# A table of issue-order rules per block, a 16-bit AND for |q| and 128-wide weight loads, in a fused attention and gated-GLU kernel

## The chip, the cores and the metric

One core of a Trainium2 chip. The metric is the device time of one execution in microseconds (us). "Ratio" always means the mean time of one kernel's fast runs over that of the other kernel's fast runs of the same rounds, so it is not quite the ratio of the medians that stand beside it.

Engines: PE is TensorE (matmuls), PEld its weight loads, DVE is VectorE, ACT is ScalarE, POOL is GpSimd, SP is the Sync engine, which issues most DMAs.

## The reference

```python
x = A_x                                    # 1 x 2048 x 640, bf16
xn = layernorm(x)
qkv = xn @ wqkv                            # 32 heads of 20
s = softmax(q @ k.T * 20**-0.5) @ v @ wo   # full attention
h = sigmoid(xn @ w_gate) * (xn @ w_up)     # 1728 wide
g = silu(h @ w_down)
return x + s * g
```

## The kernel before

Heads are worked on in groups of four and queries in chunks of 512, which makes 32 blocks. A score job is one 128 x 512 tile of scores of one head; there are 64 x 32 = 2048 of them. Either ScalarE takes a job (an exact exponential, two jobs in one 1024-column instruction from a double bank, if possible a third from a single bank) or VectorE takes it (an integer trick: one `iv` instruction per job, then three passes over groups of four jobs). All other work (projections, the GLU, the output projection) is cut into items and squeezed between the score matmuls.

The issue order of PE, ACT and DVE is fixed when the program is built. A small event model steps through time in 0.02 us, knows each engine's next free time and each buffer's, and at each step decides what to issue. Its rules are constants. This is the core of it, cut:

```python
URGENT, ROUNDS, HOLD, SLACK, LEAD, LAG, D_LAST, D_LAST_END = 0.25, 4, 0.15, 0.2, 40.0, 0.0, 20, 8
D_MAX, SLACKS = 2, (0.2, 0.2)
# ... cut
T_IV, T_ON = 0.605, 0.60                   # the model's VectorE durations
T_PASS = (0.605, 0.605, 1.15)
# ... cut: a fill of the score banks for ACT, and up to two more jobs for DVE
while len(d_new) < D_MAX and (dcur is not None or buf_free(iv_left, NIV)) \
        and busy + T_IV * len(d_new) <= T_F + T_MODE + PL + SLACKS[len(d_new)]:
    f = next((f for f in D_BANKS[own] if flex[f] <= now), None)
    # ... cut: claim a job for DVE, put its score matmul into bank f
third = next((f for f in A_BANKS[own] if flex[f] <= now), None) if len(d_new) < 2 else None
jobs = claim_act(SLOT if third is not None else SLOT - 1, [y[2][2] for y in d_new])
# ... cut: the pick on DVE
pass_ok = dve_pass and (dve_pass[0]["k"] > 0 or buf_free(pb_left, NPB))
if iv_ok and not (dve_last == "iv" and pass_ok and now < dq[0][3] + SLACK):
    nc.vector.tensor_scalar(out=d["iv"][:, j, :], in0=bank[bk], scalar1=B_OFF,
                            scalar2=0.0, op0=ALU.add, op1=ALU.max)
```

For 24 of the 32 heads q and k are projected in units of six heads (120 columns of weights), and a bound on the scores needs |q|:

```python
nc.tensor.matmul(st["ps"][0:UC, :], lhsT=wus[u][:, kd, i, :], rhs=xnT[:, c, kd, :], ...)   # UC = 120
nc.vector.scalar_tensor_tensor(out=aqs[(u, c)][0:UC, :], in0=st["q"], scalar=-1.0, in1=st["q"],
                               op0=ALU.mult, op1=ALU.max)                                  # |q|
```

After the last block a fixed sequence, the tail, divides, projects and stores the last 512 tokens.

Of the kernel before, what the change touches and what calls it, by code (L numbers as in the profile page):

```python
# [12 lines left out]
I16 = mybir.dt.int16  # L13
ACT = mybir.ActivationFunctionType
ALU = mybir.AluOpType
# [3 lines left out]
P = 128  # L19
# [8 lines left out]
UH = 6  # L28
UC = UH * DH

URGENT, ROUNDS, HOLD, SLACK, LEAD, LAG, D_LAST, D_LAST_END = 0.25, 4, 0.15, 0.2, 40.0, 0.0, 20, 8
D_ORD, M_ORD, WAIT3, FALL, M_END = 1, 0, 0.4, 1, 0.3
NPT, NPB, NIV = (3, 7), 3, 3
D_MAX, SLACKS = 2, (0.2, 0.2)
A_BANKS, D_BANKS = ((0, 1, 2), (1, 0, 2)), ((2, 1, 0), (2, 1, 0))
M_BANKS = ((2, 1, 0), (2, 1, 0))

LOG2E = 1.4426950408889634
UNIT = 128.0
# [13 lines left out]
def kernel(  # L53
# [369 lines left out]
    T_F, T_PV, T_MM, T_MODE = 0.2133, 0.2133, 0.2133, 0.107  # L423
    T_IV, T_ON = 0.605, 0.60
    T_PASS = (0.605, 0.605, 1.15)

    def t_exp(n):
        return (0.052 if n < SLOT else 0.104) + 0.4267 * n
# [4 lines left out]
    def gc(b):  # L433
        if b < PAIR:
            return divmod(b, NQC)
        return NG - 2 + (b - PAIR) % 2, (b - PAIR) // 2
# [12 lines left out]
    def mark(*e):  # L449
        return lambda t: ev_at.__setitem__(e, t)  # L450
# [56 lines left out]

    def load_wu(u):
        w = wk.tile([P, 2 * KD, GH, 32], BF16, tag="wp", bufs=2, name="wu")
        w = w.rearrange("p a j e -> p (a j e)")[:, 0:2 * KD * UC].rearrange("p (kd i f) -> p kd i f", i=2, f=UC)  # L510
        f0 = PG * GC + u * UC
        for i in range(2):
            nc.sync.dma_start(out=w[:, :, i, :], in_=wqkv_v[:, :, i, f0:f0 + UC])
        wus[u] = w

    def u_mm(st, u, i, c, kd):
        nc.tensor.matmul(st["ps"][0:UC, :], lhsT=wus[u][:, kd, i, :], rhs=xnT[:, c, kd, :],  # L517
                         start=(kd == 0), stop=(kd == KD - 1))

    def mk_ku(u, c, at):  # L520
# [31 lines left out]
    def mk_qu(u, c, at):  # L552
        st = {}

        def alloc():
            st["ps"] = misc_ps()

        def ab():
            aqs[(u, c)] = wk.tile([P, QC], BF16, tag="aq", bufs=4, name="aq")
            nc.vector.scalar_tensor_tensor(out=aqs[(u, c)][0:UC, :], in0=st["q"], scalar=-1.0, in1=st["q"],  # L560
                                           op0=ALU.mult, op1=ALU.max)

        def ev():
            st["q"] = wk.tile([P, QC], BF16, tag="ku", bufs=2, name="qu")[0:UC, :]
            nc.vector.tensor_scalar_mul(out=st["q"], in0=st["ps"][0:UC, :], scalar1=qscale)
            nc.sync.dma_start(out=qD[u][:, c * QC:(c + 1) * QC], in_=st["q"])
        return Item([("PE", alloc, [(T_MM, lambda kd=kd: u_mm(st, u, 0, c, kd)) for kd in range(KD)]),
                     ("DVE", 0.60, ev, "free", mark("qD", u, c)),
                     ("DVE", 0.60, ab, "", mark("aq", u, c))], at, pre=[("bD", u - 1)] if u else [])

    def mk_bu(u, at):
        st = {}
# [45 lines left out]
    def mk_v(pr, tts, at):  # L618
        st = {}

        def alloc():
            st["ps"] = misc_ps()

        def mm(i, kd):
            nc.tensor.matmul(st["ps"][:, i * 2 * GC:(i + 1) * 2 * GC],  # L625
                             lhsT=xn_tok(tts[i], kd),
                             rhs=wvs[pr][:, kd, :], start=(kd == 0), stop=(kd == KD - 1))

        def done(t):
            for tt in tts:  # L630
                v_at[(pr, tt)] = t
        return Item([("PE", alloc, [(0.08, lambda i=i, kd=kd: mm(i, kd)) for i in range(len(tts)) for kd in range(KD)]),
                     ("DVE", 0.065 + 0.167 * len(tts), lambda: v_evac(st["ps"], pr, tts), "free", done)], at)

    def mk_gu(c, kf, at):
# [244 lines left out]
    def buf_free(left, n):  # L880
        return len(left) < n or (left[len(left) - n][0] == 0 and left[len(left) - n][1] <= now)
# [135 lines left out]
    with tc.manual_schedule(engines={ENG.PE, ENG.Activation, ENG.DVE}):  # L1017
# [17 lines left out]
        dve_last = None  # L1035
        cur = None
        mode = None
        blk_loaded = -1
        active = []
        u_next, k_next, q_next, k_at = 0, PG, PG * NQC, {}  # L1040
# [37 lines left out]
        while chain or items or glu_items or any(it.i < len(it.ops) for it in active):  # L1078
# [2 lines left out]
            bb = base()  # L1081
            if bb > blk_loaded:
                blk_loaded = bb
                g, c = gc(bb)
                if c == 0 and g + 1 < PG:
                    spread_wst(g + 1, load_wst(g + 1))
                if c == 0 and g + 1 < NG:
                    if g % 2 == 1:
                        wvs[(g + 1) // 2] = load_wv((g + 1) // 2)
# [23 lines left out]
            for eng in ("ACT", "DVE"):  # L1113
# [47 lines left out]
                    free["DVE"] = now + 0.16  # L1161
                    continue
                iv_ok = dq and dq[0][3] <= now
                pass_ok = dve_pass and (dve_pass[0]["k"] > 0 or buf_free(pb_left, NPB))
                if iv_ok and not (dve_last == "iv" and pass_ok and now < dq[0][3] + SLACK):
                    dve_last = "iv"
                    d, j, bk, _ = dq.pop(0)
                    nc.vector.tensor_scalar(out=d["iv"][:, j, :], in0=bank[bk], scalar1=B_OFF,  # L1168
                                            scalar2=0.0, op0=ALU.add, op1=ALU.max)
                    end = now + T_IV  # L1170
                    free["DVE"] = end
                    flex[bk] = end + EL
                    d["n"] += 1
                    if d["n"] == len(d["jobs"]) and d is not dcur:
                        dve_pass.append(d)
                elif pass_ok:
                    dve_last = "pass"
                    d = dve_pass[0]
                    k = d["k"]
                    if k == 0:  # L1180
                        d["pb"] = w2.tile([P, 2, GH, QC], BF16, tag="pb", bufs=NPB, name="pb")
                        pb_left.append([2 * len(d["jobs"]), 0.0])
                        d["rel"] = (pb_left, len(pb_left) - 1)
                    passes(d, k)
                    d["k"] += 1
                    end = now + T_PASS[k]
                    free["DVE"] = end
                    if k != 1:
                        for x, (b, kt, j) in enumerate(d["jobs"]):
                            add_unit(b, kt, j, d["pb"][:, k // 2, x, :], k, end + EL, d["rel"])  # L1190
                    if k == 2:
                        dve_pass.pop(0)
                        iv_left[d["i"]][:] = [0, end]
# [13 lines left out]
            if free["PE"] <= now:  # L1207
                s = slots[nfill % 2]
                s_empty = s["a"] is None
                can_f = s_empty and s["ends"] <= now  # L1210
                dry = max(free["ACT"], now) + sum(t_exp(len(x["a"])) for x in slots if x["a"])
                margin = dry - now - (T_F + T_MODE + PL)
                us = [u for u in map(pv_pick, range(GH)) if u is not None] if oacc_at[0] <= now else []
                n_ready = min(sum(u["ready"] <= now and u["b"] == pv_block[0] for u in q) for q in pv_q)
                full = not buf_free(pt_left[3], NPT[1])
                blocked = full or not buf_free(pt_left[2], NPT[0]) or not buf_free(pb_left, NPB)
                pv_ok = len(us) == GH or (len(us) > 0 and (blocked or pv_all(pv_block[0])))
                if cur is None:
                    own = nfill % 2
                    m_new, m_bank = None, None  # L1220
                    m_it = next((e for e in active if e.i < len(e.ops) and e.ops[e.i][0] == "PE" and e.ready <= now), None)
                    if m_it is None:
                        behind = done < due() + LAG
                        for f in ((2,) if not behind and claimed[0] < NJOB * NBLK and not (FALL and not pv_ok and not can_f) else M_BANKS[own]):
                            if flex[f] <= now:
                                m_bank = f
                                break
# [12 lines left out]
                nxt = None  # L1240
                if full and pv_ok:
                    nxt = "PV"
                elif can_f and (margin < URGENT or (stay is None and not (margin > WAIT3 and any(now < flex[f] <= now + WAIT3 for f in A_BANKS[nfill % 2]) and not any(flex[f] <= now for f in A_BANKS[nfill % 2])))):
                    nxt = "F"
                elif stay is not None:
                    nxt = stay
                elif s_empty and s["ends"] <= now + HOLD and mode != "F":
                    nxt = None
                elif pv_ok and (not m_ok or full or (n_ready >= ROUNDS and done >= due() + LAG)):
                    nxt = "PV"  # L1250
                elif m_ok:
                    nxt = "M"
                if nxt == "F":
                    busy = max(0.0, free["DVE"] - now) + T_IV * len(dq)
                    own = nfill % 2
                    d_new = []
                    while len(d_new) < D_MAX and (dcur is not None or buf_free(iv_left, NIV)) \
                            and busy + T_IV * len(d_new) <= T_F + T_MODE + PL + SLACKS[len(d_new)]:
                        f = next((f for f in D_BANKS[own] if flex[f] <= now), None)
                        if f is None:  # L1260
                            break
                        x = claim_dve([t[2] for t in dcur["jobs"]] if dcur else [], [y[2][2] for y in d_new])
# [8 lines left out]
                        flex[f] = 1e9  # L1271
                        if len(dcur["jobs"]) == GH:
                            dcur = None
                    third = next((f for f in A_BANKS[own] if flex[f] <= now), None) if len(d_new) < 2 else None
                    jobs = claim_act(SLOT if third is not None else SLOT - 1, [y[2][2] for y in d_new])
                    if jobs or d_new:
                        for x, t in enumerate(jobs):
# [89 lines left out]
```

## Time and profile before

The median was 839.6 us in three runs.

| | before |
|---|---|
| busy share of ACT, PE, DVE | 96%, 94%, 91% |
| score jobs on DVE | 464 of 2048 |
| first to last exponential | 33.0 to 816.1 us |
| ACT in that stretch: needed + lost | 760.0 + 22.1 us |
| DVE in that stretch: needed + lost | 688.0 + 92.0 us |

"Needed" is an estimate: for every form of instruction on the engine, the 10th percentile of the time from its start to the next start, times its number. "Lost" is what the measured start-to-start times hold above that.

The page's first part gives busy time of each engine (share of the span, number of instructions):

```profile
span 835.7 us, 16970 instructions
...
PE 783.8 (94%) x6388; PEld 277.6 (33%) x6388; DVE 756.3 (91%) x1174; ACT 800.7 (96%) x1043; POOL 81.3 (10%) x90
```

The next view is the sum of busy time over the stretch from 60 to 780 us, in which no start or end effects lie (columns: PE, PEld, DVE, ACT, POOL, each busy us and count, then granted clock, DMA share and GB/s):

```profile
60.00:780.00 720.00, 696.51 (x5687) 239.83 (x5684) 672.46 (x1021) 716.68 (x916) 53.38 (x45) 1.00 0.25 69
```

ACT is busy 716.7 of 720 us, PE 696.5, DVE 672.5. In the names below `scA` is a double score bank, `bk` a single bank, `pt` an exponential's result, `iv` and `pb` the results of VectorE's integer trick and of its passes, `oacc` the accumulator of attention times v. The groups of instructions (busy us, mean ns of one, idle time of the engine before them and what ended it):

```profile
L83 ACT ACTIVATE pt<-scA 128x1024 bf16<-128x1024 f32 x686 | 709.0, 1181 | 6.4 <-PE bk L837 3.5 <-PE scA L837 1.8 <-PE oacc L874 0.4
L1168 DVE TENSOR_SCALAR iv<-bk 128x512 int16<-128x512 f32 x464 | 312.1, 681 | 38.8 <-PE bk L837 37.1
...
L83 ACT ACTIVATE pt<-bk 128x512 bf16<-128x512 f32 x209 | 157.5, 754 | 1.3 <-PE bk L837 1.2
...
L517 PEld LDWEIGHTS <-wu 128*120 128x120 bf16 x160 | 16.9, 131 | 19.9 <-issue 16.4 <-DMA oU<-on_bf 0.3
...
L560 DVE SCALAR_TENSOR_TENSOR aq<-qu 120x512 bf16<-120x512 bf16 x16 | 10.9, 682 | 0.2
```

The largest gap on DVE is the 38.8 us before `iv`, nearly all of it until PE had written the score bank. Between 40 and 790 us this wait is (us in total, times, longest):

```profile
DVE iv L1168 <- PE bk L837: 34.2, 59, 1.7
```

### The profile page before, as it was taken

The page shows a single profiled execution, that of the slowest core. Times are in us where ns is not written, and L with a number is a line of the kernel's source. Part 1 is how long each engine was busy: PE and PEld are TensorE (multiplying, and loading weights), DVE is VectorE, ACT ScalarE, POOL GpSimd, SP SyncE. Part 2 cuts the span into 40 slices and gives each one's busy share as a digit, 9 for nine tenths or more (in the row PEclk, how much of TensorE's full clock was granted, in tenths as well). Part 3 has the DMA queues.
Part 4 walks back from the last instruction along what each step waited for, and adds up shares of the span by engine and source line. Part 5 has one row for each costly group of instructions (what it writes and reads, how often), then busy time and mean ns, then how long its engine had stood idle before and what let it go on. Part 6 is the DMA issues. An engine that isn't in the chain of part 4 may idle for free.

```text
span 835.7 us, 16970 instructions
## 1 busy us (share of the span) xinstructions
PE 783.8 (94%) x6388; PEld 277.6 (33%) x6388; DVE 756.3 (91%) x1174; ACT 800.7 (96%) x1043; POOL 81.3 (10%) x90
## 2 busy tenths in 40 slices
PE   4799999999999999999999999999999999999985
PEld 3433223333333232333323222334333333233332
DVE  7678989999899989899899998999999899999993
ACT  7799999999999999999999999999999999999990
POOL 5000000000000000000000000000000002222041
PEclk9899999999999999999999999999999999999998
DMA  5712221122222232221113222322112222324331
GB/s 155 212 35 58 64 67 54 52 67 55 66 75 58 66 85 77 55 66 56 42 43 87 73 62 69 91 78 82 47 62 69 79 72 75 94 61 127 94 130 36
DMA packets 93587, 62.58 MB, mean 75 GB/s; under 512 B 35044, under 2 KB 86884, under 8 KB 93504
## 3 DMA queue, kind: packets, MB, share of 16 engines
q1 hardware_dynamic: 93216, 61.16, 25.9%
q8 instruction: 50, 0.82, 0.4%
q10 hardware_dynamic: 288, 0.33, 0.1%
q14 instruction: 33, 0.27, 0.1%
HBM read 46.51 MB, written 12.40 MB: 70 GB/s over the span
## 4 chain that ended last, share of the span: by engine, by line
ACT 52%; PE 26%; DVE 13%; issue 7%; DMA 1%; SPq 1%; POOLq 0%; POOL 0%; ACTq 0%; DVEq 0%
ACT pt L83 47%; PE scA L837 7%; PE oacc L874 5%; DVE iv L1168 4%; PE bk L654 4%; PE bk L692 3%; ACT tnh L83 3%; DVE pb L928 2%; DVE pb L922 2%; DVE pb L925 2%; PE bk L517 1%; PE bk L742 1%; ACT td L83 1%; PE psk L143 1%; PE bk L625 1%
## 5 line engine op out<-in xcount | busy, mean ns | idle before, releaser
L83 ACT ACTIVATE pt<-scA 128x1024 bf16<-128x1024 f32 x689 | 710.5, 1179 | 6.4 <-PE bk L837 3.5
L1168 DVE TENSOR_SCALAR iv<-bk 128x512 int16<-128x512 f32 x464 | 312.1, 681 | 38.8 <-PE bk L837 37.1
L837 PE MATMUL scA<-q,kT 32*128 32x512 bf16 x1375 | 268.6, 383 | 15.9 <-ACT pt L83 10.6
L837 PE MATMUL bk<-q,kT 32*128 32x512 bf16 x673 | 211.8, 383 | 2.0 <-DVE iv L1168 1.0
L874 PE MATMUL oacc<-pt,v 128*21 128x512 bf16 x1584 | 185.8, 383 | 0.6 <-ACT pt L83 0.4
L837 PEld LDWEIGHTS <-kT 32*128 32x128 bf16 x2048 | 85.3, 91 | 254.8 <-issue 240.3
L83 ACT ACTIVATE pt<-bk 128x512 bf16<-128x512 f32 x209 | 157.5, 754 | 1.3 <-PE bk L837 1.2
L874 PE MATMUL oacc<-pb,v 128*21 128x512 bf16 x928 | 148.4, 382 | 3.4 <-DVE pb L928 2.0
L928 DVE TENSOR_TENSOR pb<-iv,pb 128x2048 bf16<-128x2048 bf16 x116 | 149.5, 1289 | 0.6
L654 PE MATMUL bk<-xnT,wgu 128*128 128x512 bf16 x520 | 145.8, 382 | 1.6 <-DVE hT L662 0.4
L904 POOL TENSOR_TENSOR on_bf<-on,rl 128x512 bf16<-128x512 f32 x31 | 41.0, 1321 | 676.2 <-DMA rl<-rd 498.0
L692 PE MATMUL bk<-wd,hT 128*128 128x320 bf16 x448 | 85.9, 302 | 1.5 <-DVE iv L1168 0.9
L922 DVE TENSOR_SCALAR pb<-iv 128x2048 int16<-128x2048 int16 x116 | 84.0, 724 | 2.1
L874 PEld LDWEIGHTS <-v 128*21 128x21 bf16 x2512 | 51.0, 91 | 95.7 <-issue 73.1
L925 DVE TENSOR_SCALAR pb<-iv 128x2048 int16<-128x2048 int16 x116 | 82.5, 711 | 0.0
L654 PEld LDWEIGHTS <-wgu 128*128 128x128 bf16 x520 | 38.3, 97 | 66.6 <-issue 45.5
L692 PEld LDWEIGHTS <-hT 128*128 128x128 bf16 x448 | 34.5, 97 | 45.8 <-issue 37.7
L517 PE MATMUL bk<-xnT,wu 128*120 128x512 bf16 x160 | 48.7, 398 | 0.2 <-ACT pt L83 0.2
L83 ACT ACTIVATE tnh<-bk 128x512 bf16<-128x512 f32 (+1 forms) x56 | 42.7, 762 | 0.1
L662 DVE SCALAR_TENSOR_TENSOR hT<-tnh,bk 128x512 bf16<-128x512 bf16 x52 | 35.4, 680 | 5.7 <-PE bk L654 3.1
L625 PE MATMUL bk<-wv,xnT 128*128 128x160 bf16 x280 | 30.2, 243 | 1.5 <-DVE iv L1168 1.2
L752 POOL TENSOR_TENSOR xnT<-otmp,xnT 128x320 bf16<-128x320 f32 x24 | 23.3, 975 | 50.8 <-DVE otmp L749 45.3
(105 smaller groups left out, 375.4 us busy)
## 6 DMA issues: line engine op xcount, KB each, us to landing
rl<-rd SPq DMA_DIRECT2D x124, 64.0 KB
wgu<-in_B_w_gate_dram SPq DMA_DIRECT2D x24, 320.0 KB
wgu<-in_B_w_up_dram SPq DMA_DIRECT2D x24, 320.0 KB
gq_dram<-gqs SPq DMA_DIRECT2D x32, 160.0 KB
xnT<-gq_dram SPq DMA_DIRECT2D x12, 320.0 KB
xt<-in_A_x_dram SPq DMA_DIRECT2D x16, 160.0 KB
oU<-on_bf SPq DMA_DIRECT2D x108, 20.0 KB
wd<-in_B_w_down_dram SPq DMA_DIRECT2D x1, 2080.0 KB
```

Source lines behind the costliest of these rows:

```text
L83: return nc.scalar.add_instruction(mybir.InstActivation(func=func, name=nc.get_next_instruction_name(), engine=ENG.Activation, ins=[nc.sca ...
L517: nc.tensor.matmul(st["ps"][0:UC, :], lhsT=wus[u][:, kd, i, :], rhs=xnT[:, c, kd, :], start=(kd == 0), stop=(kd == KD - 1))
L625: nc.tensor.matmul(st["ps"][:, i * 2 * GC:(i + 1) * 2 * GC], lhsT=xn_tok(tts[i], kd), rhs=wvs[pr][:, kd, :], start=(kd == 0), stop=(kd == ...
L654: nc.tensor.matmul(st[key][0:fs, :], lhsT=w[:, i, kd, ko * P:ko * P + fs], rhs=xnT[:, c, kd, :], start=(kd == 0), stop=(kd == KD - 1))
L692: nc.tensor.matmul(st["ps"][:, 0:HD], lhsT=hT[0:fsz[kf], kf, t4 * P:(t4 + 1) * P], rhs=wd[0:fsz[kf], kf, h * HD:(h + 1) * HD], start=(kf = ...
L837: nc.tensor.matmul(dst, lhsT=kTs[gc(b)[0] % 2][32 * j:32 * j + 32, kt * P:(kt + 1) * P], rhs=qts[b % 3][32 * j:32 * j + 32, :], start=True ...
L874: nc.tensor.matmul(oacc[32 * j:32 * j + DH + 1, :], lhsT=lhsT, rhs=u["src"], start=first, stop=last, tile_position=(0, 32 * j), skip_group ...
L904: nc.gpsimd.tensor_tensor(out=on_bf, in0=on, in1=rl, op=ALU.mult)
L922: nc.vector.tensor_scalar(out=pb[:, 0, :, :].bitcast(I16), in0=iv, scalar1=0x7F80, scalar2=1, op0=ALU.bitwise_and, op1=ALU.bitwise_or)
L925: nc.vector.tensor_scalar(out=pb[:, 1, :, :].bitcast(I16), in0=iv, scalar1=0x007F, scalar2=0x3F00, op0=ALU.bitwise_and, op1=ALU.bitwise_or)
L928: nc.vector.tensor_tensor(out=pb[:, 1, :, :], in0=iv.bitcast(BF16), in1=pb[:, 1, :, :], op=ALU.mult)
L1168: nc.vector.tensor_scalar(out=d["iv"][:, j, :], in0=bank[bk], scalar1=B_OFF, scalar2=0.0, op0=ALU.add, op1=ALU.max)
```

## The change

Its intent: take work away from DVE and PE (two cheaper operations), make the model's picture of DVE and of the V projection truer (a dependency delay, coarser steps), and replace the constants by a row of 15 rule values for each of the 32 blocks, found by search with the event model. The core of the diff, cut:

```diff
-URGENT, ROUNDS, HOLD, SLACK, LEAD, LAG, D_LAST, D_LAST_END = 0.25, 4, 0.15, 0.2, 40.0, 0.0, 20, 8
-D_MAX, SLACKS = 2, (0.2, 0.2)
+RULE = dict(urgent=0.25, rounds=4, hold=0.15, slack=0.2, s0=0.2, s1=0.2, wait3=0.4, fall=1, lag=0.0,
+            dmax=2, third=2, dord=0, mord=0, mfew=1, npv=4)
+PLAN = (
+    (0.25, 4, 0.15, 0, 0.5, 0.2, 0.4, 1, 0.0, 2, 2, 0, 0, 1, 4),
     # ... 29 rows cut
+    (0.25, 4, 0.15, 0, 0.2, 0.2, 0.4, 1, -2.0, 2, 2, 2, 0, 1, 4),
+    (0.25, 4, 0.15, 0, 0, 0.2, 0.4, 1, -2.0, 2, 2, 2, 0, 1, 4),
+)
+    RAW = 0.115
-        nc.tensor.matmul(st["ps"][0:UC, :], lhsT=wus[u][:, kd, i, :], rhs=xnT[:, c, kd, :],
+        nc.tensor.matmul(st["ps"], lhsT=wus[u][:, kd, i, :], rhs=xnT[:, c, kd, :],      # now 128 columns
-            nc.vector.scalar_tensor_tensor(out=aqs[(u, c)][0:UC, :], in0=st["q"], scalar=-1.0, in1=st["q"],
-                                           op0=ALU.mult, op1=ALU.max)
+            nc.vector.tensor_scalar(out=aqs[(u, c)][0:UC, :].bitcast(I16), in0=st["q"].bitcast(I16), scalar1=0x7FFF,
+                                    scalar2=0, op0=ALU.bitwise_and, op1=ALU.bitwise_or)
-                     ("DVE", 0.60, ab, "", mark("aq", u, c))], ...
+                     ("DVE", 0.20, ab, "", mark("aq", u, c))], ...
     # V projection: pairs of matmuls per model step, 0.14 us, in place of single ones of 0.08
-                pass_ok = dve_pass and (dve_pass[0]["k"] > 0 or buf_free(pb_left, NPB))
+                pass_ok = dve_pass and dve_pass[0].get("at", 0.0) <= now and (...)      # waits for the RAW delay
+                rule.update(zip(KEYS, PLAN[bb]) if bb < len(PLAN) else ())
```

## The prediction

> **What bounds the kernel now.** The page gives ACT 96%, PE 94%, DVE 91% busy over 835.7 us; the chain that ended last is ACT 52%, PE 26%, DVE 13%. I split the span by the first and last exponential: start to 33 us, main part 33 to 816 us, tail of about 20 us. Stretches between 60 and 810 us show ACT 99-100% busy, so ScalarE bounds the main part. Its start-to-start pitches (trace) are 903 ns for an exponential of 1024 columns (686) and 476 ns for one of 512 (209). Adding up the 10th-percentile pitches of each form, an estimate, ACT needs 760 of the 783 us and loses only about 22. VectorE by the same count needs 688 and loses about 92, mostly before iv: the waits show 35.5 us, 61 times, for a score matmul into a bank. TensorE pays about 100 ns extra at each change of matmul kind.
>
> So time falls mainly by giving ACT less. VectorE computes 464 of the 2048 score jobs. One more job on it costs 598 + (599+599+1132)/4 = 1.18 us of DVE and saves (686x903+209x476)/1584 = 0.46 us of ACT. Before has a spare 92 us of DVE but cannot reach it, because PE serves its banks in the wrong moment.
>
> **What the change does.**
> 1. |q| by a 16-bit AND in place of the two-tensor op: 16 instructions, pitch about 600 ns. The 2048-wide AND on 16-bit data has pitch 599 ns, so 512 wide should take about 0.2 us (estimate). Saves 6-7 us of DVE, i.e. 5-6 jobs, 2.5 us of ACT.
> 2. Weights 128 instead of 120 columns wide for 160 matmuls: loads now 132 ns against 97 for the 128-wide ones, median pitch 264 against 226. The Trainium skill, "TensorE: Matmul & The Clock Gate", Weight-path perf modes, says fast weight load is on when the number of weights is 128; the trace agrees. Saves 3-6 us of PE, between 140 and 566 us. Off the critical path, worth 1 us at most.
> 3. V matmuls issued in pairs, and a 0.115 us dependency delay in the event model: no work removed; order only.
> 4. The table: more room for DVE score jobs (s0 and s1 up to 0.8 and 1.2 instead of 0.2), other bank orders, other thresholds. DVE should be fed earlier, so fewer waits of iv for PE.
>
> The table was fitted in a model, block by block, and a gain in a model only partly survives on the chip. I expect a fifth of the DVE loss (about 18 us) to be recovered; with the 7 us of |q| that is about 21 jobs, 9-10 us of ACT. ACT's own 22 us of gaps falls by 2-3. Start and tail stay. Sum: about -12 us.
>
> **Predicted: 827 us, 8 in 10 within 815 to 837.** Faster by over 2% 0.23, within 2% 0.75, slower 0.02.
>
> **What would show it.** iv count 480-490 instead of 464; ACT still 99-100% busy from 60 to 810 us; iv waiting for PE falling from 35.5 to below 25 us; aq at about 0.2 us; wu loads at 97 ns and pitch about 226; last exponential ending near 804 us; start and tail unchanged.
>
> **What would make it wrong.** If the event model tracks the chip closely, the table may recover half the DVE loss (another 10 us off). If DVE queues longer, score banks are held longer, and ACT's single-bank exponentials (209) may find no bank: more pairs without a third job, more fixed cost per exponential. If DMA landings (q, k, normalisation) slip against the model's fixed times in the new order, gaps on ACT grow and eat the gain.

## More of the kernel before

The gate's result goes to DRAM (`gq_dram`) in tiles and is read back when the output is formed. For the last four token tiles this reload (`tail_load`, four tiles of x and four of the gate's result) can only be issued after all GLU items, because it overwrites the down-projection weights `wd`.

The tail, in the chain that ended last (start us, us, what):

```profile
816.11 0.39 PE oacc L874
...
816.52 0.70 DVE on L962
...
826.29 0.34 PE bk L957 x4
...
826.66 0.70 DVE hT L999
```

The reader should keep one distance from it: the accumulator copy (`on`) starts at 816.52 us and the first instruction of the final sums (`hT`) at 826.66 us, 10.1 us later, released by PE.

## The result, and the profile after

825.9 us median (825.35 to 828.93, 4 runs) against 838.06 us for the kernel before in the same rounds: ratio 0.9862, 95% interval 0.9827 to 0.9898, so within 2%. The forecast was 827 us.

| | before | after |
|---|---|---|
| span of the profiled run | 835.7 | 823.6 us |
| score jobs on DVE | 464 | 496 |
| last exponential ends | 816.1 | 798.1 us |
| accumulator copy starts | 816.5 | 800.6 us |
| copy to first final sum | 10.1 | 14.2 us |
| ACT needed + lost | 760.0 + 22.1 | 744.1 + 20.3 us |
| DVE needed + lost | 688.0 + 92.0 | 716.9 + 47.8 us |

So the part up to the accumulator copy became 16.0 us shorter and the tail 4.0 us longer: 12 us net. (In the two other profiles of the same kernel, `after_again` and `after_yard`, the copy starts at 802.1 and 800.7 us and the distance is 14.2 and 14.0 us. So the tail's growth is steady, and the 16 us are known to about 1.5.) The page's first part, the stretch from 60 to 780 us, and the groups that answer to those of before:

```profile
span 823.6 us, 17020 instructions
...
PE 775.0 (94%) x6351; PEld 268.6 (33%) x6420; DVE 780.4 (95%) x1230; ACT 785.1 (95%) x989; POOL 85.9 (10%) x90
```

```profile
60.00:780.00 720.00, 699.40 (x5742) 234.57 (x5807) 704.84 (x1089) 716.57 (x884) 58.04 (x47) 1.00 0.25 69
```

```profile
L120 ACT ACTIVATE pt<-scA 128x1024 bf16<-128x1024 f32 x708 | 703.0, 1157 | 5.7 <-PE bk L881 3.7 <-PE scA L881 0.5 <-PE oacc L918 0.4
L1214 DVE TENSOR_SCALAR iv<-bk 128x512 int16<-128x512 f32 x496 | 330.4, 683 | 11.3 <-PE bk L881 9.9
...
L120 ACT ACTIVATE pt<-bk 128x512 bf16<-128x512 f32 x132 | 95.1, 720 | 0.3 <-PE bk L881 0.2
...
L558 PEld LDWEIGHTS <-wu 128*128 128x128 bf16 x160 | 11.0, 97 | 20.5 <-issue 16.7
...
L601 DVE TENSOR_SCALAR aq<-qu 120x512 int16<-120x512 int16 x16 | 5.5, 344 | 0.1
```

DVE went from 672.5 to 704.8 us busy in the 720 us, PE from 696.5 to 699.4, and ACT stayed at 716.6. The gap before `iv` fell from 38.8 to 11.3 us; its wait for PE between 40 and 790 us fell from 34.2 to 9.2 us:

```profile
DVE iv L1214 <- PE bk L881: 9.2, 22, 1.0
```

Weight loads of `wu` fell from 131 to 97 ns. The mean of 344 ns for |q| (`aq`) is pulled up by one record of 1194 ns; its median duration is 291 ns and the median time to the next start 199 ns. The tail, in the chain of after:

```profile
799.92 0.40 PE oacc L918 x4
800.32 1.19 PE bk L736 x8
...
810.79 0.78 PE scA L1001 x2
811.57 2.87 DMA wd<-gq_dram
...
814.71 0.70 DVE hT L1043
```

Before the final sums there now stands a DMA: the reload of the gate's result, issued at 811.57 us. And at 800.32 us, at the moment of the accumulator copy, PE still computes down-projection matmuls (`bk L736`) of the GLU, which before were done at 793 us.

### The profile page after: what moved, and what is told of

It reads as the page before. It is cut to its first block, busy times and chain, and to the rows that moved or that the text cites. A ratio compares the mean times of both kernels' runs of the same rounds, so it can differ in the third digit from the quotient of the medians.

```text
span 823.6 us, 17020 instructions
## 1 busy us (share of the span) xinstructions
PE 775.0 (94%) x6351; PEld 268.6 (33%) x6420; DVE 780.4 (95%) x1230; ACT 785.1 (95%) x989; POOL 85.9 (10%) x90
## 4 chain that ended last, share of the span: by engine, by line
PE 40%; ACT 34%; DVE 18%; issue 6%; DMA 1%; POOLq 0%; POOL 0%; SPq 0%; ACTq 0%; DVEq 0%
ACT pt L120 30%; PE scA L881 13%; PE oacc L918 8%; DVE iv L1214 7%; PE bk L698 7%; PE bk L736 5%; DVE pb L972 4%; DVE pb L966 2%; DVE pb L969 2%; PE bk L558 2%; ACT tnh L120 1%; DVE hT L706 1%; PE bk L666 1%; PE bk L881 1%; PE bk L786 1%
## 5 line engine op out<-in xcount | busy, mean ns | idle before, releaser
L1214 DVE TENSOR_SCALAR iv<-bk 128x512 int16<-128x512 f32 x496 | 330.4, 683 | 11.3 <-PE bk L881 9.9
L881 PE MATMUL scA<-q,kT 32*128 32x512 bf16 x1420 | 276.1, 382 | 11.2 <-ACT pt L120 5.8
L881 PE MATMUL bk<-q,kT 32*128 32x512 bf16 x628 | 203.4, 382 | 0.2
L918 PE MATMUL oacc<-pb,v 128*21 128x512 bf16 x992 | 156.7, 382 | 0.7 <-DVE pb L972 0.3
L972 DVE TENSOR_TENSOR pb<-iv,pb 128x2048 bf16<-128x2048 bf16 x124 | 154.5, 1246 | 0.7
L948 POOL TENSOR_TENSOR on_bf<-on,rl 128x512 bf16<-128x512 f32 x31 | 45.9, 1479 | 662.0 <-DMA rl<-rd 371.8
L120 ACT ACTIVATE pt<-bk 128x512 bf16<-128x512 f32 x132 | 95.1, 720 | 0.3 <-PE bk L881 0.2
L969 DVE TENSOR_SCALAR pb<-iv 128x2048 int16<-128x2048 int16 x124 | 91.5, 738 | 0.0
L966 DVE TENSOR_SCALAR pb<-iv 128x2048 int16<-128x2048 int16 x124 | 89.8, 724 | 1.2
L736 PE MATMUL bk<-wd,hT 128*128 128x320 bf16 x448 | 88.1, 302 | 0.9 <-DVE iv L1214 0.7
L736 PEld LDWEIGHTS <-hT 128*128 128x128 bf16 x448 | 34.1, 97 | 45.9 <-issue 37.7
L558 PE MATMUL bk<-xnT,wu 128*128 128x512 bf16 x147 | 44.4, 383 | 1.6 <-issue 0.8
```

Of the source, the lines that this page charges most:

```text
L120: return nc.scalar.add_instruction(mybir.InstActivation(func=func, name=nc.get_next_instruction_name(), engine=ENG.Activation, ins=[nc.sca ...
L558: nc.tensor.matmul(st["ps"], lhsT=wus[u][:, kd, i, :], rhs=xnT[:, c, kd, :], start=(kd == 0), stop=(kd == KD - 1))
L736: nc.tensor.matmul(st["ps"][:, 0:HD], lhsT=hT[0:fsz[kf], kf, t4 * P:(t4 + 1) * P], rhs=wd[0:fsz[kf], kf, h * HD:(h + 1) * HD], start=(kf = ...
L881: nc.tensor.matmul(dst, lhsT=kTs[gc(b)[0] % 2][32 * j:32 * j + 32, kt * P:(kt + 1) * P], rhs=qts[b % 3][32 * j:32 * j + 32, :], start=True ...
L918: nc.tensor.matmul(oacc[32 * j:32 * j + DH + 1, :], lhsT=lhsT, rhs=u["src"], start=first, stop=last, tile_position=(0, 32 * j), skip_group ...
L948: nc.gpsimd.tensor_tensor(out=on_bf, in0=on, in1=rl, op=ALU.mult)
```

## The experiments

Every variant gave correct results. In `old_abs`, `old_wu`, `old_both`, `act_more` and `tail_q` the model's durations are left alone, so the matmul, ACT and DVE sequence of after is kept and only the cost of an instruction or a DMA queue differs. In `three_only`, `table_noraw`, `more_dve` and `tail_plan` the model is run with other rules, so the sequence is another one. "Yardstick" is the kernel after, timed again in the same set. Interval is the 95% interval of the ratio to the kernel before.

| run | ratio (interval) | median us | DVE jobs | ACT needed + lost | DVE needed + lost | copy at | copy to sums |
|---|---|---|---|---|---|---|---|
| after_again | 0.9874 (0.9847 to 0.9901) | 827.15 | 496 | 744.6 + 21.2 | 717.9 + 48.2 | 802.1 | 14.2 |
| three_only | 0.998 (0.9951 to 1.0009) | 836.87 | 469 | 758.1 + 23.7 | 688.6 + 93.5 | 817.8 | 10.1 |
| old_abs | 0.9934 (0.9909 to 0.9959) | 833.15 | 496 | 744.1 + 25.8 | 724.2 + 46.0 | 806.3 | 14.0 |
| old_wu | 0.9892 (0.987 to 0.9913) | 829.67 | 496 | 744.0 + 23.3 | 717.9 + 49.8 | 803.6 | 14.0 |
| act_more | 0.991 (0.9882 to 0.9937) | 831.03 | 496 | 749.4 + 18.9 | 717.8 + 50.8 | 805.5 | 12.2 |
| table_noraw | 0.9957 (0.9928 to 0.9985) | 834.26 | 489 | 747.2 + 30.6 | 714.0 + 63.9 | 812.2 | 10.1 |
| more_dve | 1.0022 (0.9987 to 1.0057) | 838.93 | 497 | 743.4 + 32.7 | 718.6 + 58.5 | 815.1 | 11.5 |
| after_yard | 0.9859 (0.9831 to 0.9887) | 825.99 | 496 | 743.6 + 20.5 | 717.9 + 46.6 | 800.7 | 14.0 |
| tail_q | 0.9845 (0.9816 to 0.9874) | 825.18 | 496 | 744.0 + 20.2 | 717.8 + 46.8 | 800.4 | 14.2 |
| tail_plan | 0.9828 (0.98 to 0.9855) | 824.66 | 495 | 744.8 + 21.0 | 717.2 + 49.2 | 802.4 | 10.1 |
| old_both | 0.9916 (0.9888 to 0.9945) | 831.24 | 496 | 744.0 + 24.2 | 724.2 + 44.3 | 804.9 | 13.8 |

The profile columns of the `three_only` row are from `three_only_b`, the same kernel run once more; its one time was 838.57 us. (A profile of `three_only` agrees: 469 jobs, 687.9 + 94.0 us on DVE, copy at 817.4 us, 10.1 us to the sums.) The values of `after_again` and `after_yard` were worked out with one group for each line, operation, tile name and shape. Counted that way, "needed" of ACT is 0.4 to 0.6 us higher in most other rows, and "lost" as much lower; in `act_more` it is the same. The three profiles of the kernel after (800.6, 802.1, 800.7 us) also show that differences of 1.5 us in "copy at" may be mere spread.

### The table or the operations: after_again, three_only, three_only_b

`three_only` is the kernel after with an empty table, so every block runs under the constants of before:

```diff
-PLAN = ( ...32 rows... )
+PLAN = ()
```

> The changed kernel once more, as the yardstick of this set: 825 to 827 us, ratio to the kernel before 0.984 to 0.989.

> The three changes with the table emptied, so that every block runs under the old constants. My theory (ScalarE bounds the main part, and what helps is that the table lets VectorE take more score jobs): little of the gain is left, 832 to 838 us, ratio 0.993 to 1.0, iv count 460 to 475, iv waiting for PE still 25 us or more. Rival (the removed work, about 7 us of VectorE and 3 to 6 us of TensorE, makes the gain and the table adds little): 826 to 830 us, iv count 480 or more.

> The same kernel as three_only, for its profile, which the timed run did not leave. The build claims 469 score jobs for VectorE, against 464 before and 496 after. If the loss of the table's gain lies in VectorE waiting for score banks, iv still waits 25 us or more for PE and VectorE's gaps stay at 70 us or more.

Without the table a gain of 0.2% is left, and its interval includes none: 836.87 us, where the yardstick of the set had 827.15. The profile is much like that of before: 469 jobs on DVE, `iv` waiting 33.4 us for PE between 40 and 790 us (34.2 us before):

```profile
DVE iv L1181 <- PE bk L848: 33.4, 62, 2.3
```

The rival, that the removed work makes the gain by itself, fell.

### More jobs for DVE without the table: more_dve

My prediction's main mechanism was that ACT bounds the main part and that giving DVE more jobs frees it. This kernel does just that, with one constant rule:

```diff
-            ... slack=0.2, s0=0.2, s1=0.2, ...     # with PLAN = ()
+            ... slack=0.2, s0=0.5, s1=0.5, ...
```

> The three changes with an empty table, and only one constant rule changed: s0 = s1 = 0.5 instead of 0.2 in every block, so VectorE gets 497 score jobs, as many as the table gives it (496). If the number of jobs moved from ScalarE to VectorE is what pays (my prediction's step 4), 824 to 830 us. If jobs alone don't pay unless every engine is kept fed in time, 836 us or slower, with ScalarE's gaps grown by what its shorter work saves.

It gave DVE 497 jobs, one more than the table does, and ACT's need fell to 743.4 us, below that of after. Yet the time was 838.93 us, ratio 1.0022. What was saved was lost again in waits. The stretch from 60 to 780 us in this kernel, and its waits on ACT from 40 to 790 us:

```profile
60.00:780.00 720.00, 703.08 (x5728) 232.36 (x5726) 697.18 (x1079) 706.34 (x853) 56.24 (x45) 1.00 0.25 69
```

```profile
ACT pt L87 <- PE bk L848: 5.4, 14, 0.9
ACT pt L87 <- PE scA L848: 3.3, 10, 0.8
ACT pt L87 <- PE oacc L885: 2.6, 3, 1.9
```

The same view of the kernel after:

```profile
ACT pt L120 <- PE bk L881: 1.3, 4, 0.4
ACT pt L120 <- PE scA L881: 0.5, 2, 0.3
ACT pt L120 <- PE oacc L918: 0.4, 1, 0.4
```

ACT's busy time in the stretch is 706.3 us against 716.6 in after, and DVE's 697.2 against 704.8; ACT waits 11.3 us for PE (5.4 + 3.3 + 2.6) against 2.2 (before: 3.3). The number of jobs moved is not enough: the gain came where 32 jobs moved and ACT lost no more time than before (20.3 us after, 22.1 before). Here it lost 32.7.

### The same table in a slightly different model: table_noraw

```diff
-    RAW = 0.115
+    RAW = 0.0
```

> The same table and the same operations, but the event model's 0.115 us dependency delay of VectorE set to 0, so the table steers a slightly different simulation and the issue order comes out different (489 VectorE score jobs in the build). If the table holds better rules as such, most of the gain stays: 825 to 830 us. If it is fitted to one exact sequence, a small change of the model loses it: 834 to 840 us.

834.26 us, ratio 0.9957, so it lies at the edge of the second range, 834 to 840: two thirds of the gain went ((0.9957 - 0.9866)/(1 - 0.9866) is 0.68, with 0.9866 the mean of the two yardstick ratios of the other sets). DVE still took 489 jobs, but ACT lost 30.6 us and DVE 63.9. This run changes the sequence in one way only, so it doesn't say whether the delay as such makes the model better or whether any perturbation would have done the same. It does say that the rows are bound to the model they were searched in; they are not 32 better rules that hold by themselves.

### What each engine's work is worth in this sequence: old_abs, old_wu, act_more, old_both

```diff
 # old_abs: the model still counts 0.20 us
-            nc.vector.tensor_scalar(out=aqs[(u, c)][0:UC, :].bitcast(I16), ... bitwise_and ...)
+            nc.vector.scalar_tensor_tensor(out=aqs[(u, c)][0:UC, :], in0=st["q"], scalar=-1.0, in1=st["q"],
+                                           op0=ALU.mult, op1=ALU.max)
 # old_wu: 120 columns again, in the load and in the matmul
-        nc.tensor.matmul(st["ps"], lhsT=wus[u][:, kd, i, :], ...)
+        nc.tensor.matmul(st["ps"][0:UC, :], lhsT=wus[u][:, kd, i, :], ...)
 # act_more: zb is a tile of zeros
-            act_imm(st["t"][0:fs, :], st["g"][0:fs, :], ACT.Tanh, 0.5)
+            nc.scalar.activation(out=st["t"][0:fs, :], in_=st["g"][0:fs, :], func=ACT.Tanh, bias=zb[0:fs, 0:1], scale=0.5)
 # old_both: old_abs and old_wu together
```

> The changed kernel with its exact issue order, but |q| computed by the old two-tensor op (16 times about 0.6 us instead of 0.2 us, so 6.4 us more VectorE work). If VectorE is now as tight as ScalarE, 3 to 6 us slower than the changed kernel; if its remaining gaps (about 48 us by my count of pitches) absorb it, under 1.5 us slower.

> The changed kernel with its exact issue order, but the 160 projection matmuls with 120-wide weights again (about 16 to 37 ns more each, 3 to 6 us more TensorE). My theory (TensorE is not the bound): under 1.5 us slower than the changed kernel. Rival (the chain that ended last now names PE with 40%, so TensorE is the bound): 3 to 6 us slower.

> The changed kernel with its exact issue order and more ScalarE work: the 52 tanh of the gate take their zero bias from a tile; in the profile of before an exponential-length instruction with such an operand (kT) has pitch 585 ns against 477 ns without, so about 56 x 0.1 = 5 to 6 us more. If ScalarE bounds the main part: 4.5 to 6.5 us slower than the changed kernel. If TensorE or VectorE bounds it and ScalarE has slack: under 2 us slower.

> The changed kernel's exact issue order with both old operations back (|q| by the two-tensor op and 120-wide weights). If the costs add as measured one by one (about 5 us and 1.5 us): 833 to 836 us, so the order alone is worth only 2 to 5 us over the kernel before. If the order itself carries the gain: 829 us or faster.

- `old_abs` put 6.3 us on DVE (724.2 - 717.9, the yardstick of its set; 16 x (599 - 199) ns is 6.4) and cost (0.9934 - 0.9874) x 838 = 5.0 us. DVE's 48 us of lost time did not absorb it. In the trace the cost appears on ACT: its need is the same, but it lost 25.8 us where after lost 20.3.
- `act_more` put 4.8 us on ACT (52 tanh, 93 ns each on the median). The Trainium skill ("ScalarE: Activation LUTs", What ACT_TABLE_LOAD costs) says that a pointer operand adds about 93 ns; the trace agrees, 477 to 570 ns from start to start. Its set had no yardstick; against the two ratios of after in the other sets, 0.9874 and 0.9859, it cost 3.0 to 4.3 us, between the two ranges expected. Each of the intervals reaches over 2 us to either side, so it doesn't tell full cost (4.5 us or more) from most of it.
- `old_wu` put about 3.6 us on PE (mean start-to-start of neighbouring `wu` matmuls 249.6 ns, against 226.8 in `after_again`, times 160; the trace of after lacks 13 of the 160 records and cannot serve here) and cost (0.9892 - 0.9874) x 838 = 1.5 us, within the noise of the intervals. So this run cannot tell whether PE has slack: what its time is worth stays open, and it was busy 699 of the 720 us.
- `old_both` cost (0.9916 - 0.9859) x 838 = 4.8 us, less than the 5.0 + 1.5 expected, again within the intervals (831.24 us lies between the two ranges expected). It still beat the kernel before by 0.84%, about 7 us, with the same operations as before.

So in this sequence DVE is about as tight as ACT. The reading of "one bounding engine" did not hold; a microsecond added to DVE cost about 0.8 us and one added to ACT 0.6 to 0.9. One rival was not tested: the order was searched with the new durations, so part of a cost may come from disturbing a fitted sequence, and not from the engine being full. And the sum isn't one of independent parts: the operations alone are worth 0.2% under the old rules and about 0.57% in the new sequence.

### Where the tail's 4 us come from: tail_q, tail_plan, after_yard

Two explanations. Either the last store and reload stand in the Sync queue behind the five stores of the last attention result, or they are simply triggered too late. `tail_q` moves them to ACT's idle DMA queue; `tail_plan` has the rows of blocks 23 to 31 searched anew with the event model, with the added demand that the last gate results be due well before the last block ends.

```diff
 # tail_q
-            nc.sync.dma_start(out=gq_dram[tt * P:(tt + 1) * P, h * HD:(h + 1) * HD], in_=gqs)
+            eng = nc.scalar if tt >= TT - 2 and h == 1 else nc.sync
+            eng.dma_start(out=gq_dram[tt * P:(tt + 1) * P, h * HD:(h + 1) * HD], in_=gqs)
-            nc.sync.dma_start(out=tail[t4][1], in_=gq_dram[r, :])
+            nc.scalar.dma_start(out=tail[t4][1], in_=gq_dram[r, :])
 # tail_plan: 9 of 32 rows, two shown
-    (0.25, 4, 0.15, 0, 0.2, 0.2, 0.4, 1, -2.0, 2, 2, 2, 0, 1, 4),
-    (0.25, 4, 0.15, 0, 0, 0.2, 0.4, 1, -2.0, 2, 2, 2, 0, 1, 4),
+    (0.2, 4, 0.15, 0.2, 0.5, 0.5, 0.4, 0, 2.0, 1, 2, 3, 1, 3, 4),
+    (0.45, 3, 0, 0.2, 0.8, 0.2, 0.4, 1, -2.0, 2, 2, 2, 3, 3, 4),
```

> The changed kernel once more as the yardstick of this set: 825 to 829 us.

> The changed kernel with the same order on TensorE, ScalarE and VectorE, but the last two stores of the gate's result and the four loads of it for the tail issued on ScalarE's DMA queue, which is idle then, instead of behind the five oU stores on the Sync queue. If the tail grew because this store and reload came late and queued (hT waits 14.2 us after the accumulator copy instead of 10.1 us): 2 to 4 us faster than the changed kernel, first tail hT about 10.1 to 12 us after the copy. If the tail grew for another reason: no change.

> The changed kernel with the table's rows of blocks 23 to 31 searched anew so that the last gate results are due well before the last block ends (495 VectorE score jobs). If the late gate results cost the tail its 4 us: first tail hT 10.1 us after the accumulator copy, copy at 800 to 803 us, total 821 to 824 us, 2 to 5 us faster than the changed kernel. If the new rows only shift the work: 825 to 830 us.

`tail_q` did what it was meant to: the last reload was issued at 807.67 us instead of 811.57. But the final sums began at 814.57 us instead of 814.71, because that DMA now took 6.6 us instead of 2.9:

```profile
807.67 6.62 DMA wd<-gq_dram
...
814.57 0.70 DVE hT L1044
```

The windows show why (columns as above; the last two are DMA share and GB/s):

```profile
806.00:808.00 2.00, 2.00 (x13) 0.70 (x10) 0.00 (x0) 0.00 (x0) 0.00 (x0) 1.00 1.01 278
808.00:810.00 2.00, 2.00 (x11) 0.94 (x10) 0.00 (x0) 0.00 (x0) 0.00 (x0) 1.00 0.89 280
810.00:812.00 2.00, 2.00 (x9) 0.82 (x8) 0.00 (x0) 0.00 (x0) 0.00 (x0) 0.53 1.00 383
```

The 16 DMA engines are full or nearly so from 806 to 812 us: the eight loads of the tail, 4 x 320 KB + 4 x 160 KB = 1920 KB, are issued between 804.8 and 807.7 us, and the engines moved about 1880 KB in these 6 us. The queue was not the cause; my first explanation fell. The kernel before had moved most of the same bytes between 790 and 796 us, at a DMA share of up to 0.91, under cover of the last block's exponentials:

```profile
792.00:794.00 2.00, 1.99 (x14) 0.76 (x13) 2.00 (x4) 2.00 (x3) 0.00 (x0) 1.00 0.91 299
794.00:796.00 2.00, 2.00 (x19) 0.73 (x17) 2.00 (x4) 1.95 (x4) 0.00 (x0) 1.00 0.91 340
```

`tail_plan` issued all of it between 782 and 793 us. Its tail, in the chain:

```profile
802.43 0.61 DVE on L1006
...
812.10 0.34 PE bk L1001 x4
...
812.46 0.70 DVE hT L1043
```

The copy-to-sum distance is 10.1 us again (the copy starts at 802.35 us in the trace; the chain counts it from 802.43), released by PE. The copy itself came 1.8 us later (802.35 against 800.56 us), which is hardly more than the spread of the kernel after (802.1 us in `after_again`); the span is 821.4 us against 823.6. In time: 824.66 us (822.93 to 825.83) against the yardstick's 825.99 (825.3 to 829.6), ratios 0.9828 and 0.9859, about 0.3%. The intervals of the two overlap, and the expected 821 to 824 us were just missed; so the profile shows the tail mended, and the gain in time is likely but not settled. It is the fastest kernel measured, and it beats the kernel before clearly.

## Why the prediction was right or wrong

The time was right: 825.9 us against 827, well inside 815 to 837. Point by point:

1. *ACT busy 99 to 100% between 60 and 810 us:* held as far as the last exponential (716.6 of 720 us between 60 and 780 us), which ended at 798.1 us already.
2. *|q| at about 0.2 us, saving 6 to 7 us of DVE:* right in size (start to start 199 against 602 ns on the median, 16 times, is 6.4 us; in the fixed sequence DVE's need differed by 6.3 us). Its worth was not: I counted 2.5 us through ACT; in the new sequence it was worth 5.0 us, and under the old rules all the changes to operations and model together were worth about 1.7 us ((1 - 0.998) x 838; the interval reaches from nothing to 4 us).
3. *128-wide weights worth 1 us at most:* 1.5 us measured, not distinguishable from it. The Trainium skill ("TensorE: Matmul & The Clock Gate", Weight-path perf modes) says that fast weight load is on when the number of weights is 128; the loads did fall, from 131 to 97 ns in the records, which is less than the factor of about 2 that it gives (the last section has a second measure). The median pitch fell from 264 to 227 ns, but some 40% of the neighbouring `wu` matmuls had a pitch of 216 ns in both kernels, so the mean fell by only 16 to 23 ns.
4. *The table recovers a fifth (18 us) of DVE's 92 us:* DVE's loss fell by 44 us, about half, as the passage on what would make the prediction wrong had allowed for. 32 more jobs, not 21; ACT's need fell 15.9 us, not 9 to 10. `iv` waiting for PE fell to 9.2 us (40 to 790 us), far below the 25 I had set.
5. *"So time falls mainly by giving ACT less":* this step was not enough as a cause. ACT did get 15.9 us less to do, and the stretch of exponentials became 18 us shorter; but `more_dve` gave ACT as little work as the table and gained nothing. What the table adds is a sequence in which ACT loses no more time than before while DVE is fed 32 more jobs.
6. *"Start and tail stay":* the start did, the tail didn't. It grew by 4.0 us, because the last down projections run after the last exponential (at 800.32 us in the chain, against 798.1) and the 1920 KB reload behind them finds no cover.

So two sizes were off in opposite directions: the main part shortened by 16 us where I had 12, and the tail gave 4 us back where I had none. The sum was right partly for that reason, and that part was luck.

One fear in the prediction was the wrong way round. The single-bank exponentials did fall, from 209 to 132, but a pair costs ACT 903 ns, 452 ns a job, and a single one 476 ns, so fewer of them cost ACT nothing.

## What to carry to other kernels

When three engines are each over 90% busy, don't rely on finding one that bounds: fix the sequence, add a few microseconds to one engine at a time, and read what each is worth. A table searched in a model belongs to that model, down to a delay of 0.1 us, and a search can pay with whatever it isn't asked to spare; here with the reload after the loop, which cost 4 us on the chip. Put the end of the program into the objective before searching.

## What the Trainium skill lacked or had wrong

- "Perfetto Trace Analysis", Identifying the Most-Contended Engine, says to optimize the engine of the highest occupancy first. Here that was ACT (96%). Moving work from it to DVE by one constant (`more_dve`: ACT's need 760.0 to 743.4 us) left the time at 1.0022, and after the change 6.3 us more on DVE cost 5.0 us. The section has no test for two engines that are tight together.
- "VectorE: DVE Perf Modes", The DRAIN you can't avoid, gives no cost of a read after write on the same engine. A third pass right behind the second, whose result it reads, started 718 ns after it (median of 17 pairs in before, 719 ns in after); with another job's `iv` behind the second pass, the next start came after 600 ns (73 times in before), and a third pass behind an `iv` started after 601 ns. So about 118 ns, near the 0.115 us that the change put into its model.
- The same page's tier table has no row for `scalar_tensor_tensor`. On 512 bf16 elements from SBUF its start-to-start time was 602 ns (median of 16), the `tensor_scalar` AND's 199 ns.
- "TensorE: Matmul & The Clock Gate", LDWEIGHTS, gives columns / 1.2 as the nanoseconds of a load, so 100 ns for 120 columns. The trace has 132 ns (median of 160) for 120 columns and 97 ns for 128. These durations hold a large fixed part: loads of 6, 21 and 80 columns took 81, 90 and 116 ns. Over half of the neighbouring `wu` loads started closer together than a matmul takes, 51 to 52 ns apart with 120 columns and 15 ns with 128. By either count a column of the loads under 128 columns cost 0.43 to 0.45 ns here, not 0.83.
